# Attention and two feed-forward layers on one core: first chunk's scores in fp32, weight shifts given one half ahead, bit steps off the layer change

## The chip, the cores and the metric

One core of a Trainium2 chip runs the whole program. The metric is device time in microseconds (us), from the profiler's view of one execution; lower is better.

## The reference

```python
# _attn_ref: q, k, v are (4, 12, 448, 64), w_pre and w_post (12, 12)
scores = (1 / sqrt(64)) * matmul(q, k.transpose(0, 1, 3, 2))
scores = einsum('bhij,hg->bgij', scores, w_pre)
attn = exp(scores - max(scores, axis=-1)); attn = attn / (sum(attn, axis=-1) + 1e-09)
attn = einsum('bhij,hg->bgij', attn, w_post)
x = matmul(attn, v)                      # then to (1792, 768)
# _moe_ref: w_in (768, 2048), w_out (2048, 768)
h = x @ w_in; x = (h * cos(h)) @ w_out
# _moe2_ref: w_gate, w_val (768, 1536), w_out (1536, 768)
g = x @ w_gate; out = (g / (1 + exp(-g)) * (x @ w_val)) @ w_out
```

## The kernel before

**Attention.** Each of the four batches has its 448 query rows cut into four chunks of 12, 12, 11 and 10 blocks of ten rows. For a chunk, `qk` makes the scores of a pair of heads `m` (two heads, in rows 0 to 63 and 64 to 127 of the array) as three matmuls a head on values split into a rounded high part and a rest (type fp32r): `hi_q`, `lo_q`, `hi_k` and `lo_k` make these parts. `spread` copies each head's scores out of PSUM and sends them by DMA into `X`, where the partitions are ten rows times twelve heads, so that one matmul with a 120 by 120 matrix (`premix`, tile `psm`) mixes the heads of a block. Then come row maximum (`rowmax`, DVE), exponential (`expo`, ACT), normalization, the second mixing (`post`, tile `psa`) and, once a chunk is done, the product with v (`pv`, tile `psv`).

What a step does is written out by hand: a plan holds, for each block (a step), the functions to be called, and `ORDER` sorts them within a step. `QK_FIRST` and `V_FIRST` are steps of chunk 0, at which the pairs of heads of chunk 1 are scored and the four parts of v are loaded. Engines run their instructions in the order in which they are recorded, so an instruction that waits holds back all behind it on its engine.

Ahead of step 0 stands a start written out by hand: loads of K and q on SP's queue, splits, the scores of chunk 0, their copies, and the spreads. A spread of chunk 0 goes in two DMAs, the first for blocks 0 to 3 (`FIRST`), the second for blocks 4 to 11; SP and ACT issue them.

**Feed-forward.** A unit (layer, group of 256 hidden columns, quarter `t` of the tokens) makes its hidden values (`l1`, tiles `ph`; `hidden_a`, `hidden_b`) while the unit before it is multiplied into the output (`l2`, tiles `py`, six column blocks `m`). `acc` is summed by DVE, or copied by ACT in a layer's first group. Weights arrive as 64-bit numbers and are turned to fp32 halves: `w_shift` (ACT) scales the high words, three `w_bits` steps (DVE) put in the low ones, `w_split` (ACT and POOL) makes high part and rest. `w_steps` lists these; `fill(n)` runs the next n entries between the matmuls' other work. Halves of the out matrix and of the in matrices are two kinds of conversion, and a list of one kind (`what`) is followed by one of the other. At the end of layer 0 the maxima of `acc` give the scale of layer 1 (`next_max`, `next_unit`, `next_part`).

Of the kernel before, what the change touches and what calls it, by code (L numbers as in the profile page):

```python
# [7 lines left out]
F32 = mybir.dt.float32  # L8
F32R = mybir.dt.float32r
# [21 lines left out]
Q_STEPS = (-10, -6, -3)  # L31
K_STEPS = (1, 3, 5, 8, 10, 12)
V_STEPS = (4, 8, 12, 16)
QK_FIRST = (0, 0, 3, 3, 5, 5)
V_FIRST = (8, 10, 12, 14)
AT_DVE = (2, 5, 8)
ORDER = (
    "scale_v", "mixed_out", "l1_part", "norm_hi", "dma_v", "spread", "post", "rowmax", "w_sum",
# [16 lines left out]
def attention(ctx, tc, qT, kT, vN, mix, xs, ff):  # L55
    nc = tc.nc
# [27 lines left out]
    def bank(name):  # L84

        second = len(banks) % 4 > 1 or "closed" in banks
        banks.append(name)
        pool, tag = (ps_v, "pv") if second else (ps_s, "s")
        return pool.tile([128, 512], F32, tag=tag, name=name)
# [40 lines left out]
    def hi_k(b, m, copy=nc.scalar.copy):  # L130

        t = ktiles[b, m] = tuple(
            p_k.tile([128, S], F32R, tag=f"k{z}", name=f"k{z}_{b}_{m}") for z in range(2)
        )
        copy(t[0], raws["k", b, m])
# [5 lines left out]
    def dma_q(b, c, parts=(slice(0, 6),)):  # L141

        if parts[0].start == 0:
            qtiles[b, c] = tuple(
                p_q.tile([128, 6, 120], F32R, tag=f"q{z}", name=f"q{z}_{b}_{c}") for z in range(2)
            )
            raws["q", b, c] = p_q.tile([128, 6, 120], F32, tag="qr", bufs=2, name=f"qr_{b}_{c}")
        src = qT[b, c].rearrange("d (m i) -> d m i", m=6)
        for s in parts:
            nc.sync.dma_start(raws["q", b, c][:, s], src[:, s])  # L150
# [40 lines left out]

    X, SP, SMALL, PM, E, EHL, PA, AT, PV = ({} for _ in range(9))

    def qk(b, c, m, places=()):

        n = 10 * CH[c]
        for e in range(2):
            name = f"pss_{b}_{c}_{2 * m + e}"
            if places:
                pool, tag = places[(2 * m + e) % len(places)]  # L200
                SP[b, c, 2 * m + e] = pool.tile([128, 512], F32, tag=tag, name=name)
            else:
                SP[b, c, 2 * m + e] = bank(name)
        for i, (zq, zk) in enumerate(((0, 0), (1, 0), (0, 1))):
            for e in range(2):
                r = slice(64 * e, 64 * e + 64)
                nc.tensor.matmul(  # L207
                    SP[b, c, 2 * m + e][:n, :S], qtiles[b, c][zq][r, m, :n], ktiles[b, m][zk][r],
                    start=(i == 0), stop=(i == 2),
                )  # L210

    def spread_part(b, c, h, k0, k1):

        eng = nc.scalar if h % 2 else nc.sync
        eng.dma_start(X[b, c][h:120:12, k0:k1], raws["s", h][10 * k0:10 * k1])

    def spread(b, c, h, pool=p_s, bufs=None, copy=nc.scalar.copy):
# [166 lines left out]
    with tc.manual_schedule():  # L384
        vec, act, pl = nc.vector, nc.scalar, nc.gpsimd
        dma_k(0, 0, p_fk)
        dma_q(0, 0, (slice(0, 3),))
        dma_k(0, 1, p_fk)
        dma_q(0, 0, (slice(3, 6),))
        for m in range(2, 6):  # L390
            dma_k(0, m, p_fk)
        nc.sync.dma_start(mix_sb, mix)
        dma_q(0, 1)
        places = (ps_s, "s"), (ps_a, "a"), (ps_m, "m")
        for m in range(6):
            hi_k(0, m, act.copy if m % 2 else vec.tensor_copy)
            lo_k(0, m, pl if m % 2 else vec)
            if m < 2:
                hi_q(0, 0, m, act.copy)
                lo_q(0, 0, m, pl if m else vec)  # L400
        wpre_sb = const.tile([120, 120], F32, name="wpre_sb")
        nc.vector.tensor_scalar(wpre_sb, wpre_raw, SM, None, op0=ALU.mult)
        for m in range(6):
            qk(0, 0, m, places)
            for e in range(2):
                spread(0, 0, 2 * m + e, p_fk, 12, vec.tensor_copy if e else act.copy)
        for h in range(H):
            spread_part(0, 0, h, FIRST, CH[0])
        wm = p_small.tile([120, 1], F32, tag="wm", bufs=1, name="wm")
        nc.vector.tensor_reduce(out=wm, in_=wp, axis=AX.X, op=ALU.max, apply_absolute_value=True)  # L410
        wpost_sb = [const.tile([120, 120], F16, name=f"wpost{z}") for z in range(2)]
        first_k.close()
        p_at = pool("a_at", 2)
        p_o = pool("a_o", 3)
        pw = pow2_c(pow2_b(pow2_a(wm, 120, "w"), 120, "w"), 120, "w")
        nc.vector.tensor_scalar(wpost_sb[0], wp, pw[:120, 1:2], None, op0=ALU.mult)
        nc.vector.scalar_tensor_tensor(
            wpost_sb[1], wp, pw[:120, 1:2], wpost_sb[0], op0=ALU.mult, op1=ALU.subtract
        )
        for e in range(2):  # L420
            hi_q(0, 1, e)
            lo_q(0, 1, e)
        for i in range(-1, NB + 24):
            if i == first[B - 1, 3]:
                scores.close()
                banks.append("closed")
                ff.open_early()
            if i == NB + 1:
                mixed.close()
                ff.open_ps()  # L430
            for kind in ORDER:
                for fn, a in plan.pop((i, kind), []):
                    fn(*a)
# [3 lines left out]
class FeedForward:  # L437
# [180 lines left out]
    def w_steps(self):  # L618


        halves = lambda keys: [(key, z) for key in keys for z in range(2)]
        groups = [(L, g) for L in range(2) for g in range((FF1, FF2)[L] // 256)]
        outs = lambda L, g: [((L, "o", 2 * g + e), z) for z in range(2) for e in range(2)]
        seq = [("conv", outs(0, 0), 0, ("o", 0, 0))]
        for n in range(1, len(groups) + 1):
            for bi, batch in enumerate(self.batches(*groups[n]) if n < len(groups) else [()]):

                room = 4 * (n - 3) if n < 8 else 24 if n == 8 else 4 * (n - 1)
                if batch:
                    seq.append(("max", batch, room, None))  # L630
                if bi == 0 and n > 1:
                    seq.append(("conv", outs(*groups[n - 1]), 4 * (n - 2) + 1, ("o", *groups[n - 1])))
                if batch:
                    seq.append(("conv", halves(batch), room, ("i", *groups[n], bi)))
        self.to_load = []
        out = []
        for kind, what, room, name in seq:
            if kind == "max":
                hs = halves(what)
                for j, (key, z) in enumerate(hs):  # L640
                    out.append((room, None, [
                        *([(self.new_scale, what)] if j == 0 else []), (self.w_max, key, z),
                        *([(self.w_sum, what), (self.add_sum, what)] if j == 3 else []),
                    ]))
                continue
            self.to_load += what
            for j, (key, z) in enumerate(what):
                nxt = what[j + 1] if j + 1 < len(what) else None
                for k in range(3):
                    do = [(self.w_shift, key, z)] if j == k == 0 else []  # L650
                    do.append((self.w_bits, key, z, (k,)))
                    if k == 1 and nxt:
                        do.append((self.w_shift, *nxt))
                    if k == 2:
                        do += [(self.w_split, key, z), (self.load_next,)]
                    out.append((room, name if nxt is None and k == 2 else None, do, key))
        return out

    def add_sum(self, batch):
# [14 lines left out]
    def fill(self, n):  # L674

        while n and self.todo:
            room, name, do, *key = self.todo[0]
            if room > self.now or (key and any(key[0] in batch for batch in self.sums)):
                return
            self.todo.pop(0)  # L680
            for fn, *a in do:
                fn(*a)
            if name:
                self.done.add(name)
            n -= 1
# [162 lines left out]
    def steps(self):  # L848
# [7 lines left out]
        for i in range(1, len(seq) + 1):  # L856
# [31 lines left out]
                self.l1(0, 0, 2, 0)  # L888
            for m in range(6):
                self.l2(L0, g0, t0, m)  # L890
                if i == 1 and m == 0:
                    self.hidden(0, 0, 1, 1)
                if m == 0 and 1 < i < len(seq):
                    self.fill(1)
                    self.hidden_b(L, g, t, 1)
                    self.sum_up()
                if m in (1, 3) or i == 1 or (m == 5 and (L0 or i < 4)):
                    self.fill(1)
                if 0 <= t_max < 4 and m == 3:
                    self.next_unit(t_max)  # L900
                if 0 < m < 4 and 0 <= t_new < 4:
                    self.next_part(t_new, m + 2)
# [77 lines left out]
```

## Time and profile before

| | us |
|---|---|
| median of 3 runs | 1418.13 (1417.9 to 1418.47) |
| the profiled execution | 1418.45 |
| its span, first to last instruction | 1416.7 |
| PE matmuls busy in the span | 1385.8 (98%) |
| DVE, ACT, POOL busy | 993.4, 621.0, 469.5 |

The span is what the trace shows; 1.75 us of the execution lie outside it. PE's share counts a matmul's modelled duration, in which neighbours overlap, so 98% doesn't mean that PE works at its peak. Names such as `pss<-k,q` are output and inputs of an instruction; L207 is line 207 of the kernel; ACTq and SPq are the queues' own issue instructions, x12 the number of merged instructions.

### The profile page before, as it was taken

The numbers are of one execution on the slowest core, as the hardware profiler recorded it, in microseconds if no ns is written. First come the engines' busy times: TensorE is split into PE (matmuls) and PEld (weight loads), VectorE is DVE, ScalarE is ACT, GpSimd is POOL, SyncE is SP. The second block draws the span as 40 slices with busy tenths as digits, with TensorE's granted clock in tenths as the row PEclk, the third lists the DMA queues.
The fourth block names the chain that finished last, engine by engine and source line by source line (L and its number), as shares of the span: only waits on it lengthen the run. The fifth ranks groups of instructions, "written<-read, shape, count | busy, mean of one in ns | idle before, by whom it ended". The sixth has DMA issues, their size and how long they took to land.

```text
span 1416.7 us, 25084 instructions
## 1 busy us (share of the span) xinstructions
PE 1385.8 (98%) x9562; PEld 964.0 (68%) x9562; DVE 993.4 (70%) x2157; ACT 621.0 (44%) x1319; POOL 469.5 (33%) x499
## 2 busy tenths in 40 slices
PE   6899999999999999999999999999999999999998
PEld 3577777777776776767676767656666666666666
DVE  4977887877879667878887878875555466465523
ACT  3776776777665543333333333455422232232210
POOL 2454454453423332333242333343322222231310
PEclk9999999999999999999999999999999999999999
DMA  5554554554547222221121221021212122120012
GB/s 175 153 155 129 153 157 127 165 156 119 162 121 246 56 68 67 67 68 56 57 78 56 58 77 45 23 67 46 78 35 66 46 61 74 45 78 12 1 47 111
DMA packets 100209, 126.16 MB, mean 89 GB/s; under 512 B 29592, under 2 KB 88440, under 8 KB 100088
## 3 DMA queue, kind: packets, MB, share of 16 engines
q1 hardware_dynamic: 99248, 123.26, 29.4%
q8 instruction: 75, 1.23, 0.4%
q10 hardware_dynamic: 840, 1.29, 0.3%
q14 instruction: 46, 0.38, 0.1%
HBM read 75.45 MB, written 10.37 MB: 61 GB/s over the span
## 4 chain that ended last, share of the span: by engine, by line
PE 83%; DVE 9%; DMA 3%; ACT 2%; issue 2%; ACTq 1%; POOL 0%; SPq 0%; DVEq 0%; POOLq 0%
PE ph L718 12%; PE ph L720 12%; PE ph L719 12%; PE py L768 9%; PE py L769 8%; PE py L770 8%; PE psm L232 8%; PE psv L306 4%; PE pss L207 4%; PE psa L281 2%; PE psa L282 2%; PE psa L283 2%; DMA x<-s 2%; DVE el L268 1%; DVE sm L237 1%
## 5 line engine op out<-in xcount | busy, mean ns | idle before, releaser
L718 PE MATMUL ph<-x,h_i 128*128 128x448 f16 x960 | 338.7, 353 | 0.0
L720 PE MATMUL ph<-x,l_i 128*128 128x448 f16 x960 | 338.3, 352 | 0.0
L719 PE MATMUL ph<-x,h_i 128*128 128x448 f16 x960 | 338.3, 352 | 0.0
L774 DVE TENSOR_TENSOR acc<-py,acc 128x448 f32<-128x448 f32 x288 | 177.5, 620 | 143.0 <-PE py L770 133.7
L753 POOL TENSOR_TENSOR gl<-r,gh 128x448 fp32r<-128x448 f32 x112 | 135.0, 1205 | 401.7 <-ACT gh L752 398.1
L768 PE MATMUL py<-gh,h_o 128*128 128x448 f32 x672 | 254.7, 379 | 6.9 <-DVE acc L774 4.8
L769 PE MATMUL py<-gl,h_o 128*128 128x448 f32 x672 | 243.9, 363 | 0.0
L770 PE MATMUL py<-gh,l_o 128*128 128x448 f32 x672 | 243.6, 362 | 0.0
L261 POOL TENSOR_SCALAR eh<-e,sm 120x448 f16<-120x448 f32 x180 | 122.0, 678 | 245.3 <-DVE sm L256 155.2
L232 PE MATMUL psm<-x,wpre_sb 120*120 120x448 f32 x360 | 179.6, 582 | 4.5 <-ACT e L245 4.2
L718 PEld LDWEIGHTS <-h_i 128*128 128x128 f16 x960 | 93.8, 98 | 91.2 <-issue 8.8
L245 ACT ACTIVATE e<-psm,sm 120x448 f32<-120x448 f32 x180 | 114.8, 638 | 89.3 <-DVE sm L237 81.0
L720 PEld LDWEIGHTS <-l_i 128*128 128x128 f16 x960 | 93.9, 98 | 87.6
L719 PEld LDWEIGHTS <-h_i 128*128 128x128 f16 x960 | 94.0, 98 | 82.2 <-issue 0.3
L768 PEld LDWEIGHTS py<-gh,h_o 128*128 128x128 f32 x672 | 126.3, 188 | 24.5 <-DVE acc L774 8.2
L237 DVE TENSOR_REDUCE sm<-psm 120x1 f32<-120x448 f32 x180 | 111.0, 617 | 41.9 <-PE psm L232 41.7
L751 DVE SCALAR_TENSOR_TENSOR r<-ph,by_i,r 128x448 f32<-128x448 f32 x112 | 76.3, 681 | 90.4 <-PE ph L720 73.6
L752 ACT CAST gh<-r 128x448 fp32r<-128x448 f32 x112 | 63.5, 567 | 164.9 <-DVE r L751 164.2
L268 DVE SCALAR_TENSOR_TENSOR el<-e,sm,eh 120x448 f16<-120x448 f32 x180 | 135.6, 753 | 0.0
L770 PEld LDWEIGHTS py<-gh,l_o 128*128 128x128 f32 x672 | 126.1, 188 | 8.9
L769 PEld LDWEIGHTS py<-gl,h_o 128*128 128x128 f32 x672 | 126.3, 188 | 7.5
L592 POOL TENSOR_TENSOR l_i<-f_i,h_i 128x384 f16<-128x384 f32 x80 | 78.1, 976 | 160.0 <-ACT h_i L591 160.0
(102 smaller groups left out, 2235.7 us busy)
## 6 DMA issues: line engine op xcount, KB each, us to landing
r_o<-in_w_out SPq DMA_DIRECT2D x56, 384.0 KB
x<-s SPq DMA_DIRECT2D x84, 210.0 KB
r_i<-in_w_in SPq DMA_DIRECT2D x32, 384.0 KB
x<-s SPq DMA_DIRECT2D x48, 192.5 KB
r_i<-in_w_gate SPq DMA_DIRECT2D x24, 384.0 KB
r_i<-in_w_val SPq DMA_DIRECT2D x24, 384.0 KB
x<-s SPq DMA_DIRECT2D x48, 175.0 KB
qr<-in_qT SPq DMA_DIRECT2D x15, 360.0 KB
```

The source lines that it names most:

```text
L232: nc.tensor.matmul(ps[:120, :S], wpre_sb, X[b, c][:120, k], start=True, stop=True)
L237: nc.vector.tensor_reduce(out=sm[:, 0:1], in_=PM[b, c, k][:120, :S], axis=AX.X, op=ALU.max, negate=True)
L261: nc.gpsimd.tensor_scalar(eh, E[b, c, k], sm[:, 3:4], 1.0, op0=ALU.mult, op1=ALU.mult)
L268: nc.vector.scalar_tensor_tensor(el, E.pop((b, c, k)), sm[:, 3:4], eh, op0=ALU.mult, op1=ALU.subtract)
L718: nc.tensor.matmul(ps, wh, xh, start=(kk == 0), stop=False)
L719: nc.tensor.matmul(ps, wh, xl, start=False, stop=False)
L720: nc.tensor.matmul(ps, wl, xh, start=False, stop=(kk == 5))
L753: nc.gpsimd.tensor_tensor(gl, r, f(gh), op=ALU.subtract)
L768: nc.tensor.matmul(ps, wh, gh[:, e], start=(e == 0), stop=False)
L769: nc.tensor.matmul(ps, wh, gl[:, e], start=False, stop=False)
L770: nc.tensor.matmul(ps, wl, gh[:, e], start=False, stop=(e == 1))
L774: nc.vector.tensor_tensor(acc, ps, acc, op=ALU.add)
```

## The change

1. The scores of chunk 0 of batch 0 are made by a new `qk_first` from the raw q and K, one fp32 matmul a head in place of three fp32r ones. The splits of that chunk's q are gone. Those of K stay for the later chunks: all high parts on DVE, all rests on POOL.
2. In the start, scores, K's high part and copies follow each other pair by pair. ACT issues the spreads that it copied itself (even heads), SP those of DVE. The split of chunk 1's q comes ahead of the scale of `w_post`.
3. The pairs of chunk 1 are scored at steps 1, 4 and 7 in place of 0, 3 and 5; the first load of v is recorded at step 11 in place of 8.
4. In `w_steps`, the shift of the next half is given at the second bit step also where the next half is of the other kind.
5. In units that follow the last of layer 0 (`0 <= t_max < 4`) no `fill` stands after `m` 1 and 3.
6. In the first unit `hidden(0, 0, 1, 1)` is cut in two, `hidden_a` behind block 0 and `hidden_b` behind block 3.

```diff
-QK_FIRST = (0, 0, 3, 3, 5, 5)
-V_FIRST = (8, 10, 12, 14)
+QK_FIRST = (1, 1, 4, 4, 7, 7)
+V_FIRST = (11, 12, 13, 14)
...
+    def qk_first(m, places):
+
+        for e in range(2):
+            pool, tag = places[(2 * m + e) % len(places)]
+            ps = SP[0, 0, 2 * m + e] = pool.tile([128, 512], F32, tag=tag, name=f"pss_0_0_{2 * m + e}")
+            r = slice(64 * e, 64 * e + 64)
+            nc.tensor.matmul(
+                ps[:120, :S], raws["q", 0, 0][r, m], raws["k", 0, m][r], start=True, stop=True
+            )
...
-        eng = nc.scalar if h % 2 else nc.sync
+        eng = nc.sync if h % 2 else nc.scalar
...
         for m in range(6):
-            hi_k(0, m, act.copy if m % 2 else vec.tensor_copy)
-            lo_k(0, m, pl if m % 2 else vec)
-            if m < 2:
-                hi_q(0, 0, m, act.copy)
-                lo_q(0, 0, m, pl if m else vec)
+            qk_first(m, places)
+            hi_k(0, m, vec.tensor_copy)
+            for e in range(2):
+                spread(0, 0, 2 * m + e, p_fk, 12, vec.tensor_copy if e else act.copy)
+            lo_k(0, m)
...
+                    if k == 1:
+                        nxt = self.to_load[n] if n < len(self.to_load) else None
+                        given = nxt and (not last or nxt[0][1] == "o" or seq[si + 1][0] == "conv")
+                        if given:
+                            keys.append(nxt[0])
+                            do.append((self.w_shift, *nxt))
...
-                if i == 1 and m == 0:
-                    self.hidden(0, 0, 1, 1)
+                if i == 1 and m in (0, 3):
+                    (self.hidden_b if m else self.hidden_a)(0, 0, 1, 1)
...
-                if m in (1, 3) or i == 1 or (m == 5 and (L0 or i < 4)):
+                if m in (1, 3) and not 0 <= t_max < 4 or i == 1 or (m == 5 and (L0 or i < 4)):
                     self.fill(1)
```

ACT at the start of the program, before (`s_0_2` is the copied score of chunk 0, head 2; `10x4x448` is the first DMA of a head, `10x8x448` the second):

```order
L135 CAST k_0_5_164<-kr_5_133 128x448
L223 COPY s_0_0_179<-pss_0_0_170 120x448
L215 DMA x_0_178<-s_0_1_182 10x4x448
L223 COPY s_0_2_193<-pss_0_2_185 120x448
L215 DMA x_0_178<-s_0_3_196 10x4x448
```

and of the change:

```order
L229 ACT_TABLE_LOAD
L229 COPY s_0_0_146<-pss_0_0_138 120x448
L221 DMA x_0_145<-s_0_0_146 10x4x448
L229 COPY s_0_2_160<-pss_0_2_153 120x448
L221 DMA x_0_145<-s_0_2_160 10x4x448
```

Five casts ahead of the first copy are gone, and each DMA now follows a copy of ACT's own.

ACT where the conversions pass from an in matrix to an out matrix in layer 0, before (`f_i`, `f_o` are halves in work, `py_0_2_3` is group 0, quarter 2, block 3; `hpi` marks the sine):

```order
L772 COPY acc_7798<-py_0_2_1_8108 128x448
L772 COPY acc_7798<-py_0_2_2_8117 128x448
L772 COPY acc_7798<-py_0_2_3_8125 128x448
L591 CAST h_i_3_0_8063<-f_i_3_1_8057 128x384
L772 COPY acc_7798<-py_0_2_4_8138 128x448
L772 COPY acc_7798<-py_0_2_5_8146 128x448
L741 ACTIVATE r_1_0_0_8183<-r_1_0_0_8183,hpi 128x448
L553 ACTIVATE f_o_0_8188<-r_o_0_7806 128x384
```

and of the change:

```order
L779 COPY acc_7768<-py_0_2_1_8078 128x448
L555 ACTIVATE f_o_0_8087<-r_o_0_7776 128x384
L779 COPY acc_7768<-py_0_2_2_8089 128x448
L779 COPY acc_7768<-py_0_2_3_8097 128x448
L593 CAST h_i_3_0_8033<-f_i_3_1_8027 128x384
L779 COPY acc_7768<-py_0_2_4_8110 128x448
L779 COPY acc_7768<-py_0_2_5_8118 128x448
L748 ACTIVATE r_1_0_0_8155<-r_1_0_0_8155,hpi 128x448
```

The shift of the first out half (`f_o_0`) stands ahead of the last in half's cast now, and no longer behind the next unit's sine.

DVE in the last unit of layer 0 (group 7, quarter 3), before (`f_o` steps are bit steps of weights, `mx` the maxima, `sx` the sum over partitions that `next_unit` reads):

```order
L774 TENSOR_TENSOR acc_7799<-py_7_3_1_12006,acc_7799 128x448
L778 TENSOR_REDUCE mx_11998<-acc_7799 128x1
L567 SCALAR_TENSOR_TENSOR f_o_1_11933<-r_o_1_11278,f_o_1_11933 128x384
L774 TENSOR_TENSOR acc_7799<-py_7_3_2_12024,acc_7799 128x448
L778 TENSOR_REDUCE mx_11998<-acc_7799 128x1
L774 TENSOR_TENSOR acc_7799<-py_7_3_3_12037,acc_7799 128x448
L778 TENSOR_REDUCE mx_11998<-acc_7799 128x1
L561 TENSOR_SCALAR f_o_1_12001<-f_o_1_12001 128x384
L796 TENSOR_SCALAR mx_11789<-sx_12047 128x1
```

and of the change:

```order
L781 TENSOR_TENSOR acc_7769<-py_7_3_1_11976,acc_7769 128x448
L785 TENSOR_REDUCE mx_11968<-acc_7769 128x1
L781 TENSOR_TENSOR acc_7769<-py_7_3_2_11989,acc_7769 128x448
L785 TENSOR_REDUCE mx_11968<-acc_7769 128x1
L781 TENSOR_TENSOR acc_7769<-py_7_3_3_12002,acc_7769 128x448
L785 TENSOR_REDUCE mx_11968<-acc_7769 128x1
L803 TENSOR_SCALAR mx_11761<-sx_12011 128x1
```

The two bit steps between the sums have moved to the next unit.

## Rows read from the trace of the kernel before

**Rows 1.** the page: the span of the profiled execution

```profile
span 1416.7 us, 25084 instructions
```

**Rows 2.** waits of PE: for whom, us in total, times, longest

```profile
PE py L768 <- DVE acc L774: 4.8, 7, 0.9
PE py L768 <- ACT acc L772: 1.9, 3, 1.3
```

**Rows 3.** timeline of ACT: start, us, what, [idle before <-releaser]

```profile
3.79 0.49 ACT L154 CAST q<-qr 128x360 fp32r<-128x360 f32 x1 [1.77 <-DMA qr<-in_qT]
9.19 0.56 ACT L135 CAST k<-kr 128x448 fp32r<-128x448 f32 x1 [1.38 <-DMA kr<-in_kT]
13.85 0.78 ACTq L215 DMA_DIRECT2D x<-s  x1
17.73 8.06 ACTq L215 DMA_DIRECT2D x<-s  x7
25.84 1.84 ACT L223 COPY s<-pss 120x448 f32<-120x448 f32 x4 [7.87 <-DMA x<-s]
```

**Rows 4.** timeline of PE, start of the program

```profile
24.40 3.34 PE L232 MATMUL psm<-x,wpre_sb 120*120 120x448 f32 x4
32.41 1.76 PE L232 MATMUL psm<-x,wpre_sb 120*120 120x448 f32 x4
34.11 1.47 PE L207 MATMUL pss<-k,q 64*120 64x448 f32 x12
```

**Rows 5.** chain that ended last, mixing of the heads

```profile
254.12 4.27 PE psv L306 x96
```

**Rows 6.** timeline of DVE at the start: two casts of K

```profile
3.36 0.39 DVE L135 CAST k<-kr 128x448 fp32r<-128x448 f32 x1 [2.10 <-DMA kr<-in_kT]
8.91 1.32 DVE L135 CAST k<-kr 128x448 fp32r<-128x448 f32 x1
```

**Rows 7.** timeline of PE: mix of the first block of chunk 1

```profile
48.05 1.01 PE L232 MATMUL psm<-x,wpre_sb 120*120 120x448 f32 x2
```

**Rows 8.** timeline of ACT while chunk 0 is mixed

```profile
30.89 0.63 ACT L245 ACTIVATE e<-psm,sm 120x448 f32<-120x448 f32 x1 [1.73 <-DVE sm L237]
37.85 0.53 ACT L223 COPY s<-pss 120x448 f32<-120x448 f32 x1 [0.71 <-DMA x<-s]
```

**Rows 9.** timeline of DVE in chunk 1: a maximum over v

```profile
49.90 0.93 DVE L169 TENSOR_REDUCE vmx<-v 112x1 f32<-112x768 f32 x1
```

**Rows 10.** chain that ended last, at a chunk's end

```profile
169.89 4.53 DMA x<-s
```

**Rows 11.** timelines of PE and ACT, first unit of the feed-forward part

```profile
474.59 0.47 PE L768 MATMUL py<-gh,h_o 128*128 128x448 f32 x1 [1.31 <-ACT acc L772]
...
473.54 0.56 ACT L752 CAST gh<-r 128x448 fp32r<-128x448 f32 x1 [0.75 <-DVE r L751]
```

**Rows 12.** timelines of DVE (two) and PE where a shift comes late

```profile
526.92 0.74 DVE L561 TENSOR_SCALAR f_i<-f_i 128x384 int32<-128x384 int32 x1 [0.58 <-ACT f_i L553]
...
556.47 0.36 DVE L561 TENSOR_SCALAR f_o<-f_o 128x384 int32<-128x384 int32 x1 [0.70 <-ACT f_o L553]
...
558.00 0.47 PE L768 MATMUL py<-gh,h_o 128*128 128x448 f32 x1 [0.71 <-DVE acc L774]
```

**Rows 13.** timelines of DVE and PE at the change of layer

```profile
920.87 1.15 DVE L567 SCALAR_TENSOR_TENSOR f_o<-r_o,f_o 128x384 int32<-128x384 int32 x1
924.30 0.76 DVE L561 TENSOR_SCALAR f_o<-f_o 128x384 int32<-128x384 int32 x1
...
922.60 0.47 PE L768 MATMUL py<-gh,h_o 128*128 128x448 f32 x1 [0.28 <-DVE acc L774]
925.18 0.16 PE L533 MATMUL su_i<-u_i,ones 128*128 128x2 bf16 x1 [1.10 <-DVE mx L796]
```

**Rows 14.** one stretch: its us, then busy PE, PEld, DVE, ACT, POOL

```profile
560.00:700.00 140.00, 139.29 (x718) 100.63 (x717) 115.99 (x223) 49.14 (x88) 47.29 (x44) 1.00 0.24 68
```

**Rows 15.** timeline of ACT: a shift that waits for POOL

```profile
913.32 0.56 ACT L553 ACTIVATE f_o<-r_o 128x384 f32<-128x384 f32 x1 [2.10 <-POOL l_o L592]
```

More of the change, by code (lines that the diff above doesn't have):

```diff
@@ L143, in dma_q @@
         if parts[0].start == 0:
-            qtiles[b, c] = tuple(
-                p_q.tile([128, 6, 120], F32R, tag=f"q{z}", name=f"q{z}_{b}_{c}") for z in range(2)
-            )
+            if b + c:
+                qtiles[b, c] = tuple(
+                    p_q.tile([128, 6, 120], F32R, tag=f"q{z}", name=f"q{z}_{b}_{c}") for z in range(2)
+                )
             raws["q", b, c] = p_q.tile([128, 6, 120], F32, tag="qr", bufs=2, name=f"qr_{b}_{c}")
@@ L192, in attention, with qk @@
     X, SP, SMALL, PM, E, EHL, PA, AT, PV = ({} for _ in range(9))
-    def qk(b, c, m, places=()):
+    def qk_first(m, places):
[5 more added lines that the diff above has]
+                ps[:120, :S], raws["q", 0, 0][r, m], raws["k", 0, m][r], start=True, stop=True
+            )
+    def qk(b, c, m):
         n = 10 * CH[c]
         for e in range(2):
[L198 to L203, printed above, removed]
+            SP[b, c, 2 * m + e] = bank(f"pss_{b}_{c}_{2 * m + e}")
         for i, (zq, zk) in enumerate(((0, 0), (1, 0), (0, 1))):
@@ L395, in attention @@
         for m in range(6):
-            hi_k(0, m, act.copy if m % 2 else vec.tensor_copy)
-            lo_k(0, m, pl if m % 2 else vec)
-            if m < 2:
-                hi_q(0, 0, m, act.copy)
-                lo_q(0, 0, m, pl if m else vec)
+            qk_first(m, places)
[3 more added lines that the diff above has]
+            lo_k(0, m)
         wpre_sb = const.tile([120, 120], F32, name="wpre_sb")
         nc.vector.tensor_scalar(wpre_sb, wpre_raw, SM, None, op0=ALU.mult)
[L403 to L406, printed above, removed]
         for h in range(H):
             spread_part(0, 0, h, FIRST, CH[0])
+        for e in range(2):
+            hi_q(0, 1, e)
+            lo_q(0, 1, e)
         wm = p_small.tile([120, 1], F32, tag="wm", bufs=1, name="wm")
@@ L419, in attention @@
         )
-        for e in range(2):
-            hi_q(0, 1, e)
-            lo_q(0, 1, e)
         for i in range(-1, NB + 24):
@@ L634, in w_steps @@
                     seq.append(("conv", halves(batch), room, ("i", *groups[n], bi)))
-        self.to_load = []
-        out = []
-        for kind, what, room, name in seq:
+        self.to_load = [half for kind, what, *_ in seq if kind == "conv" for half in what]
+        out, n, given = [], 0, False
+        for si, (kind, what, room, name) in enumerate(seq):
             if kind == "max":
@@ L645, in w_steps @@
                 continue
-            self.to_load += what
             for j, (key, z) in enumerate(what):
-                nxt = what[j + 1] if j + 1 < len(what) else None
+                n += 1
                 for k in range(3):
-                    do = [(self.w_shift, key, z)] if j == k == 0 else []
+                    keys = [key]
+                    last = j == len(what) - 1
+                    do = [] if given or k else [(self.w_shift, key, z)]
                     do.append((self.w_bits, key, z, (k,)))
-                    if k == 1 and nxt:
-                        do.append((self.w_shift, *nxt))
+                    if k == 1:
[4 more added lines that the diff above has]
+                            do.append((self.w_shift, *nxt))
                     if k == 2:
                         do += [(self.w_split, key, z), (self.load_next,)]
-                    out.append((room, name if nxt is None and k == 2 else None, do, key))
+                    out.append((room, name if last and k == 2 else None, do, *keys))
         return out
@@ L676, in fill @@
         while n and self.todo:
-            room, name, do, *key = self.todo[0]
-            if room > self.now or (key and any(key[0] in batch for batch in self.sums)):
+            room, name, do, *keys = self.todo[0]
+            if room > self.now or any(key in batch for key in keys for batch in self.sums):
                 return
```

## The prediction

> **What bounds the kernel now.** I read the page first: the span is 1416.7 us [rows 1], and PE is busy nearly throughout. So an edit pays only where PE waits or runs slowly. The waits of PE come next. In the feed-forward part its output matmuls (L768) wait for the sums of DVE seven times, 4.8 us in all, and for the copies of ACT three times, 1.9 us [rows 2]. With the 1.1 us in which the sum matmul of a weight scale stands behind the layer change [rows 13], that is 7.8 us, and it is all that edits 4 to 6 can give back. The rest of what the change touches is the start.
>
> There the timelines say what ends last. ACT has the first half of q at 3.79 us and the last block of K at 9.19 [rows 3]; the inputs are all there early. But from 17.73 to 25.79 ACT's queue does nothing except issue seven spreads, 1.15 us each, and the copies behind them begin at 25.84 [rows 3]. The exponentials of chunk 0 stand behind those copies. The first block of chunk 1 is mixed at 48.05 [rows 7]. From 25.84 to there are 22.2 us, in which ACT again stands idle, for example 1.73 us for a row maximum and 0.71 us for a spread that still holds a buffer [rows 8]. After 48 us the same work follows in the same order, on PE; I take the whole rest to move with that moment.
>
> One more view belongs to the start, the matmul durations. Two mixes take 3.34 us at 24.40 and 1.76 us at 32.41 [rows 4]. So PE runs at the lower of its two levels, 1.2 GHz, up to about 32 us, and at 2.4 GHz after it.
>
> **Start: scores in fp32.** A pair is two fp32 matmuls over 64 rows, which no row of before shows. The nearest ones: an fp32 mix of the same 448 columns takes 1.67 us at the lower level and 0.88 at the upper (half of [rows 4]). Whether the two halves of a pair run side by side is open. In fp32r they do: twelve matmuls of 448 columns in 1.47 us [rows 4] are 0.12 us each, where one alone at 2.4 GHz needs 448/2.4 = 0.187. In fp32 the product with v, two heads in two halves of the columns, takes 4.27 us for 96 records, that is 48 matmuls of 120 columns [rows 5]; scaled from the mix (0.88 us for 448 columns) they would need 11.3 us one by one. Both rows speak for side by side. So a pair costs 1.67 us (bounds 0.88, and 3.34 if one by one).
>
> The Trainium skill ("TensorEngine Tiling (Array Packing)", Key Properties) says the same: tiles of the array work independently, but a change of the tiling mode drains the engine. By it the switch from pairs to the full-height matmuls that follow would cost one drain, as it did before the change.
>
> The first pair can start at 3.8 us. Six at 1.67 us end at 13.8; with the upper level from the middle on, 3.8 + 3 x 1.67 + 3 x 0.88 = 11.5. Then ACT copies the last even head (0.46 us, a quarter of the 1.84 of [rows 3]) and issues its spread (0.78 us): 12.7 to 15.1, middle 13.9. Its six second spreads follow, at 1.15 us each 6.9 us. **ACT is free at 20.8 us (19.6 to 22.0) in place of 25.84: 5.0 us (3.8 to 6.2).** The first block's maximum isn't later: a spread lands within 4.53 us [rows 10], so the last first part at 14.3 + 4.5 = 18.8; with a mix at 1.67 and a maximum at about 0.6 (block rows of DVE) that is 21.1, just beside 20.8.
>
> The splits that go (q) and move (K) lie beside this. A cast of K takes 0.39 us on DVE when nothing runs on POOL, and 1.32 us when POOL subtracts beside it [rows 6]. Each DVE turn of cast and copy is then 0.39 + 0.6 = 1.0 us, or 1.9 us. The first hides behind a pair of 1.67 us; the second doesn't, and six turns of it would end at 3.4 + 11.4 = 14.8 in place of 14.3, which costs 0.5 us. I take nothing, since POOL subtracts only what DVE has cast, so that a rest runs mostly beside a copy from PSUM. The Trainium skill ("GPSIMD Engine Reference", Specifications) speaks against the change here: POOL shares its SBUF interfaces with VectorE and contends with instructions in a two-port mode, and all six rests are on POOL now. The trace agrees as to size (0.39 against 1.32); by the rule alone all casts would be slow, and the sum 0.5 us smaller.
>
> **From ACT's freedom to chunk 1.** The same work remains, except that the four first copies now stand behind the first exponential. What can go are the waits: the pairs of chunk 1 come at steps 1, 4 and 7, evenly, so a buffer is no longer asked for before its spread has landed (0.71 us here), and PE, at work on scores from 5 us on, should reach the upper level before 32 us, which shortens the 1.73 us. Bounds 0 and 4, taken 2.0, less than the 2.4 of the two rows. Against it stands the load of v: its four maxima, 0.93 us each [rows 9], fall on four steps in a row in place of every second one. The SP queue's order isn't changed by step 11; the DMAs have landed anyway. DVE has some slack over chunk 1, so 0 to 1.9 us, taken 0.3. **Start: 5.0 + 2.0 - 0.3 = 6.7 us.**
>
> **First unit, edit 6.** PE waits 1.31 us for a copy of ACT, because the cast of `gh`, queued ahead of that copy, waits 0.75 us for DVE [rows 11]. With `hidden_b` behind block 3, two copies go ahead of the cast. The sine stays ahead, so a little of the wait remains: 1.2 us (0.7 to 1.9, all of ACT's waits). What `hidden_b` feeds is needed only in the next unit, behind 18 matmuls.
>
> **Shifts, edit 4.** The hand-overs between kinds are 25; four of them meet a moment at which DVE has nothing else. There its bit step waits 0.58 or 0.70 us for ACT's shift, the hidden values behind it are late, the sum behind those too, and PE waits 0.71 us [rows 12]. Two more such pairs, near 656 and 755 us, read as the second does. With the shift one half ahead these waits go: 0.58 + 3 x 0.70 = 2.7 us (0 if ACT stands elsewhere then, up to DVE's 4.8 [rows 2] less the next term).
>
> **Layer change, edit 5.** Bit steps of 1.15 and 0.76 us stand between sums; PE waits 0.28 us for the next sum and 1.10 us for the maxima read behind the second [rows 13]. Without them 1.4 us (0 to 1.9). The steps then stand in the next unit, where DVE waits for PE.
>
> **The sum** is 6.7 + 1.2 + 2.7 + 1.4 = 12.0 us. The profiled execution has 1418.45 us, 0.3 above the median; against the median 1418.1 - 12.0 = **1406.1 us**.
>
> **Rivals.** *One by one:* the halves of a pair don't overlap. Against it speak [rows 4, 5]. With the upper level from the third pair on, 3.8 + 2 x 3.34 + 4 x 1.76 = 17.5, then 0.46 + 0.78 + 6.9: ACT is free at 25.6, and the start gives 0.2 + 2.0 - 0.3 = 1.9 us; total 7.2, 1411. With no rise of the clock 3.8 + 20.0 + 8.1 = 31.9: 6.1 lost, the whole 0.9 slower, 1419.
>
> *The shifts don't pay:* what DVE waited for it waits for still, in another instruction. Then only the start and edits 5 and 6 give: 9.3 us, 1408.8; with none of edits 4 to 6, 1411.4.
>
> *Late spreads of chunk 1:* its last copies stand at step 8 of 12, two steps later than before. A spread needs up to 4.53 us from issue to landing and then is the chain that ends last [rows 10]. If PE waits for it at step 12, up to 3 us are given back: 1409.
>
> *Slower:* a shift given ahead needs one of two buffers that POOL frees. At 913 us ACT waits 2.10 us for that [rows 15], and all behind it on ACT, `gh` and copies, waits too. If each of the 25 hand-overs put 0.5 us on PE: 12.5 lost, 2.7 not gained, 9.3 gained, 1418.1 + 3.2 = 1421. It decides from 9.3/25 = 0.37 us each. Against it: shifts inside a kind are given just so already, and from 560 to 700 us PE is busy 139.29 of 140 us [rows 14].
>
> **How the numbers follow.** Less than 0.2% (2.8 us) can't be told from no change here. Forecast, 1401 to 1410: 0.68. One by one: 0.10, of it 0.02 slow enough to be the same. The shifts don't pay: 0.09. Late spreads: 0.06. Slower: 0.04; no effect at all for reasons I don't see: 0.03, split into same and slower. Faster is then 0.92, same 0.04, slower 0.04. The low end, 1400, is all upper bounds of the start (6.2 + 4 = 10.2) and some 8 us of waits; the high end, 1412, takes in the first two rivals. About 0.08 lie above it and 0.06 below.
>
> **What would show it.** Right: ACT's first copy of chunk 1 or first exponential at 20 to 22 us; a pair of fp32 scores with two starts nearly together; the first mix of chunk 1 near 41 us; no wait of bit steps for ACT near 550, 650 and 750 us (earlier by the start); PE's waits for DVE's sums below 2.5 us, the one before the scale's sum gone. Wrong: second spreads that take longer on a fuller queue, since the inputs and spreads now meet; PE at 1.2 GHz long into chunk 0; a wait of PE for DVE in chunk 1 as large as what the start gave.

## The result and the profile after

| | before | changed |
|---|---|---|
| median of 5 runs, us | 1418.29 (1417.9 to 1421.75) | 1405.65 (1404.97 to 1407.2) |
| ratio to before, 95% interval | | 0.9909 [0.9895, 0.9922] |
| the profiled execution, its span | 1418.45, 1416.7 | 1407.2, 1405.4 |
| first exponential (ACT) | 27.54 | 21.90 |
| first mix of chunk 1 (PE) | 48.05 | 43.96 |
| first and last output matmul | 467.42, 1412.71 | 463.50, 1401.46 |
| feed-forward part between these | 945.29 | 937.96 |

The kernel became 12.6 us faster, 0.9%; 1406.1 was forecast. The profiled execution is the longest of the five, 1.55 us above the median.

The start in ACT's timeline (start, us, what, idle before and what ended it):

```profile
5.73 0.53 ACT L229 COPY s<-pss 120x448 f32<-120x448 f32 x1 [3.71 <-PE pss L201]
...
13.24 0.53 ACT L229 COPY s<-pss 120x448 f32<-120x448 f32 x1 [0.85 <-ACT s L229]
13.80 8.04 ACTq L221 DMA_DIRECT2D x<-s  x7
21.90 0.63 ACT L251 ACTIVATE e<-psm,sm 120x448 f32<-120x448 f32 x1 [8.13 <-DMA x<-s]
```

ACT is done issuing at 21.84, where [rows 3] had 25.79; now the first exponential comes next, and no copy stands ahead of it. The same stretch in PE's timeline, and SP's queue:

```profile
3.87 6.98 PE L201 MATMUL pss<-kr,qr 64*120 64x448 f32 x24 [3.87 <-DMA qr<-in_qT]
15.39 0.75 PE L105 MATMUL psp_w<-diag_w,ones 120*128 120x120 f32 x2 [4.54 <-DVE diag_w L100]
17.17 1.82 PE L238 MATMUL psm<-x,wpre_sb 120*120 120x448 f32 x2 [1.02 <-DMA x<-s]
...
43.96 0.98 PE L238 MATMUL psm<-x,wpre_sb 120*120 120x448 f32 x2 [2.21 <-DMA v<-in_vN]
...
45.41 1.78 PE L238 MATMUL psm<-x,wpre_sb 120*120 120x448 f32 x2
```

```profile
27.91 10.70 SPq L231 DMA_DIRECT2D x<-s  x8
38.66 2.11 SPq L163 DMA_DIRECT2D v<-in_vN  x4
```

The twelve fp32 matmuls of the scores take 6.98 us, so the halves of a pair run side by side (one by one, at the 0.88 us of a mix at 2.4 GHz, they would need 10.6); in the trace the two start 0.01 to 0.03 us apart. The first mix of chunk 1 then waits 2.21 us. The row names the load of v, but this matmul reads `x`: its last spread is issued at 38.61, v right behind it, and by the semaphore updates in the trace that spread lands at 43.72. Against [rows 7] the mix comes 4.1 us earlier, where 7.0 were forecast. And the mix behind it (one matmul, recorded as two) takes 1.78 us. The stretches (us, busy PE, PEld, DVE, ACT, POOL, granted clock, DMA share, GB/s) say why:

```profile
15.00:22.00 7.00, 5.58 (x18) 3.01 (x18) 2.40 (x9) 0.10 (x1) 1.07 (x2) 0.53 0.61 193
22.00:44.00 22.00, 16.94 (x131) 10.37 (x129) 16.51 (x46) 15.71 (x41) 9.37 (x13) 1.00 0.65 191
44.00:49.00 5.00, 5.00 (x32) 3.42 (x34) 3.18 (x9) 1.91 (x5) 0.99 (x3) 0.66 0.78 210
```

Twice PE waits some microseconds and then works at 1.2 GHz for a while: at the end of the 4.54 us before 15.39 and on from there, and behind the 2.21 us before 43.96.

In the feed-forward part PE's waits up to 900 us, and the two places of [rows 11] and [rows 13], now read (PE's rows):

```profile
PE py L775 <- DVE acc L781: 1.5, 2, 0.9
PE py L775 <- ACT acc L779: 0.5, 1, 0.5
```

```profile
467.90 0.47 PE L775 MATMUL py<-gh,h_o 128*128 128x448 f32 x1 [0.47 <-ACT acc L779]
...
914.60 0.16 PE L535 MATMUL su_i<-u_i,ones 128*128 128x2 bf16 x1
```

From 900 to 970 us no wait of PE is left. Up to 900 us bit steps wait for a shift 5 times in place of 16, and not at all from 490 to 850 us, as here on DVE:

```profile
549.26 0.35 DVE L563 TENSOR_SCALAR f_o<-f_o 128x384 int32<-128x384 int32 x1
```

The part is 7.3 us shorter, where 5.3 were forecast. So the sum was right by two errors that nearly cancel, and the experiments ask about both.

### The profile page after: what moved, and what is told of

Its sections match the earlier page's. It is cut to its first block, busy times and chain, and to the rows that moved or that the text cites. A ratio compares the mean times of both kernels' runs of the same rounds, so it can differ in the third digit from the quotient of the medians.

```text
span 1405.4 us, 25058 instructions
## 1 busy us (share of the span) xinstructions
PE 1379.4 (98%) x9550; PEld 960.8 (68%) x9550; DVE 990.4 (70%) x2156; ACT 618.6 (44%) x1314; POOL 471.7 (34%) x501
## 4 chain that ended last, share of the span: by engine, by line
PE 90%; DVE 5%; ACT 1%; DMA 1%; issue 1%; ACTq 1%; POOL 0%; SPq 0%; DVEq 0%; POOLq 0%
PE ph L725 13%; PE ph L727 12%; PE ph L726 12%; PE py L775 9%; PE py L776 9%; PE py L777 9%; PE psm L238 9%; PE psv L312 5%; PE pss L213 4%; PE psa L287 2%; PE psa L289 2%; PE psa L288 2%; DVE el L274 1%; DVE sm L243 1%; DMA qr<-in_qT 1%
```

## The experiments

Ratios are to the kernel before, run on the same chip, with 95% intervals. "Theory A" and "B" are those of each expectation.

**1. The parts alone, on the kernel before.** Four kernels: edits 1 to 3 without the feed-forward edits; edits 4 to 6 alone; edit 4 alone (`w_steps` and `fill` as in the diff ahead of the prediction); edit 5 alone:

```diff
-                if m in (1, 3) or i == 1 or (m == 5 and (L0 or i < 4)):
+                if m in (1, 3) and not 0 <= t_max < 4 or i == 1 or (m == 5 and (L0 or i < 4)):
```

Edits 1 to 3: 

> Edits 1 to 3 alone; the feed-forward part is that of before. Theory A (read from the trace after: the start gives 4.0 us at the first mix of chunk 1, the feed-forward edits 7.3): 4.0 us faster than before, about 1414.3, and the first output matmul of the feed-forward part near 463.5 as in the trace after. Theory B (the prediction's terms, start 6.7 and the feed-forward edits 5.3): 1411.6. If the wait before the first mix of chunk 1 and the stretch at 1.2 GHz behind it come from the start's own order, both stand here too, near 42 to 44 and 45 to 49 us.

Edits 4 to 6: 

> Edits 4 to 6 alone; the start is that of before. Theory A: 7.3 us faster, about 1411.0. Theory B: 5.3 us faster, 1413.0. Rival, a part of the 7.3 is not the edits' own but the clock's or an unrelated difference between two executions: between 5 and 6.5 us. The feed-forward part from its first output matmul to its last should take 938.0 us as in the trace after under A, 940.0 under B, where before takes 945.3.

Edit 4: 

> Edit 4 alone, shifts given one half ahead across kinds. Theory A: the four late shifts give 3.4 us and a little at the layer change, 1414.5. Theory B (the prediction's term): 2.7 us, 1415.6. Rival of the prediction, the shifts don't pay: 1418.3, with the waits of bit steps still there or moved to another instruction. The late sum before the output matmuls near 527, 558, 656 and 756 us should be gone; the one near 550 may leave 0.1.

Edit 5: 

> Edit 5 alone, no fill after m 1 and 3 in the units after the last of layer 0. Theory A: 2.3 us faster, 1416.0 (waits of 0.3 near 922.6, of 1.1 ahead of the scale's sum and of some 0.9 behind the change go). Theory B (the prediction's term): 1.4 us, 1416.9. Rival: the bit steps are late in the next unit, nothing is gained, 1418.3.

| kernel | median, us | ratio | first to last output matmul, us |
|---|---|---|---|
| edits 1 to 3 | 1412.47 | 0.996 [0.9948, 0.9972] | 945.33 |
| edits 4 to 6 | 1410.31 | 0.9947 [0.9935, 0.9959] | 938.27 |
| edit 4 | 1413.56 | 0.997 [0.996, 0.9981] | 941.02 |
| edit 5 | 1415.75 | 0.9986 [0.9977, 0.9996] | 942.89 |
| before, same chip | 1417.88 | | 945.29 (first profile) |

The start gives 5.4 us and the feed-forward edits 7.6, together 13.0; both theories had one of the two wrong: the start is between 4.0 and 6.7. The profile of edits 1 to 3 has the wait ahead of chunk 1 (1.82 us, first mix at 42.58) and the stretch at 1.2 GHz behind it as well, so both come from the start's own order. The last column leaves the start out: 7.0 us for the three edits, 4.3 for edit 4, 2.4 for edit 5. In edit 4's kernel PE's first unit still waits as in [rows 11], with all three edits that wait is gone (PE's timelines, edit 4 first, then edits 4 to 6):

```profile
470.95 0.47 PE L773 MATMUL py<-gh,h_o 128*128 128x448 f32 x1 [0.45 <-ACT acc L777]
473.74 0.47 PE L773 MATMUL py<-gh,h_o 128*128 128x448 f32 x1 [1.32 <-ACT acc L777]
```

```profile
471.08 0.47 PE L773 MATMUL py<-gh,h_o 128*128 128x448 f32 x1 [0.45 <-ACT acc L777]
```

For a finer account I set the 2016 starts of output matmuls of two traces side by side, each counted from its first. The changed kernel gains 1.30 us in the first unit (edit 6), 1.13, 0.76, 0.76 and 0.76 in the 5th, 7th, 14th and 21st (edit 4, and the same places in its kernel alone), 1.74 in the 32nd, the last of layer 0 (edit 5), and 0.61 in the 33rd. This last gain appears with edit 4 alone (0.53) and with edit 5 alone (0.51): either one suffices. Before, two output matmuls start 0.29 us late there, one behind a copy of ACT; why either edit mends it stayed open.

PE's waits up to 900 us in edit 5's kernel are those of [rows 2] (4.5 of 4.8 us for DVE fall there), in edit 4's 1.5:

```profile
PE py L768 <- DVE acc L774: 4.5, 6, 0.9
```

```profile
PE py L773 <- DVE acc L779: 1.5, 2, 0.9
```

**2. fp32 alone, on the kernel before.** `qk_first` in place of `qk(0, 0, m, places)`, without `hi_q` and `lo_q` of that chunk:

```diff
-            qk(0, 0, m, places)
+            qk_first(m, places)
```

> The kernel before with the first chunk's scores in fp32 and no split of its q; splits of K, copies and spreads stand in the order of before. Theory A, the order in which ACT and DVE work is what held ACT back and fp32 alone gives little: the casts and rests of K still stand ahead of DVE's copies to 11.6 us, six copies of 0.6 us follow, ACT's last copy ends near 15.5 and its seven issues near 23.5; the first exponential near 23.6 in place of 25.8, 2.2 us or less faster. Theory B, the matmuls were the bound: all of the 4.0 us at the first exponential come from fp32, near 21.9.

1417.87 us, 0.9999 [0.9991, 1.0008]: nothing. (A single profile says less: this one begins chunk 1 at 46.77, 1.3 us earlier than before, but then takes 946.74 us from the first to the last output matmul, where the same code before took 945.29; PE falls to 1.2 GHz there once, at 472 us behind the wait of [rows 11].) ACT, then DVE:

```profile
13.32 0.53 ACT L233 COPY s<-pss 120x448 f32<-120x448 f32 x1 [3.31 <-DVE s L233]
...
17.98 7.84 ACTq L225 DMA_DIRECT2D x<-s  x7
25.86 1.84 ACT L233 COPY s<-pss 120x448 f32<-120x448 f32 x4 [8.02 <-DMA x<-s]
```

```profile
8.83 1.44 DVE L139 TENSOR_TENSOR k<-kr,k 128x448 fp32r<-128x448 f32 x1
10.19 1.14 DVE L409 TENSOR_SCALAR wpre_sb<-mix_sb 120x120 f32<-120x120 f32 x1
11.26 1.67 DVE L233 COPY s<-pss 120x448 f32<-120x448 f32 x3
```

DVE's first copy still stands behind the rests of K, to 11.26; ACT issues spreads of DVE's copies and waits for them; it is free at 25.86, as before to 0.02 us. My 23.5 was too early: the score banks stay full until DVE copies, and PE makes its last five score matmuls only from 11.92 on, in 5.33 us, at 1.2 GHz (granted clock 0.50 from 11.5 to 32 us). So theory A holds more strongly than I put it: in the old order fp32 gives nothing. That it pays because the scores no longer need the splits, so that the order of edit 2 becomes possible, is the reading this leaves; it isn't shown, since no run has that order without fp32, and the clock has a part in the late copies here.

**3. The wait before chunk 1.** Three changes of the changed kernel: v two steps later; the last pairs at step 6; all loads of v behind the first spreads of chunk 2.

```diff
-V_FIRST = (11, 12, 13, 14)
+V_FIRST = (13, 14, 15, 16)
```

> The changed kernel with the loads of v two steps later (13, 14, 15, 16). Theory A, v's 1.4 MB, issued right behind the last spread of chunk 1, share the DMA engines with it: PE's wait of 2.21 us ahead of chunk 1's first mix falls by 1 us or more, and with it the stretch at 1.2 GHz behind it goes, 1.5 us: 1 to 3 us faster than the changed kernel. Theory B, the spread is late by its own issue (37.85 to 38.61) and takes its 4.5 us anyway: wait unchanged within 0.3 us, time unchanged.

```diff
-QK_FIRST = (1, 1, 4, 4, 7, 7)
+QK_FIRST = (1, 1, 4, 4, 6, 6)
```

> The changed kernel with the last two pairs of chunk 1 scored at step 6 in place of 7. Theory A (late spreads): the last spread is issued some 1.5 us earlier, the wait of 2.21 us ahead of chunk 1's first mix falls to about 0.7 us, and the stretch at 1.2 GHz goes or shrinks: 1.5 to 3 us faster than the changed kernel. Theory B (buffers): the copies then stand behind spreads that still hold the six buffers, ACT waits instead and the exponentials are as much later: no change.

```diff
-V_FIRST = (11, 12, 13, 14)
+V_FIRST = (13, 14, 15, 16)
...
-                at(v0, dma_v, b, jc)
+                at(v0 if b else V_FIRST[3], dma_v, b, jc)
```

> The changed kernel with all four loads of v recorded at step 16, behind the first spreads of chunk 2, and the maxima at steps 17 to 20: on SP's queue no load of v follows chunk 1's last spread directly. Theory A, v's traffic delays that spread: PE's wait ahead of chunk 1's first mix (2.21 us in the changed kernel, 1.85 with two of the four loads behind it) falls to 1 us or less. Theory B, the spread is issued too late and takes its 4.5 to 5 us: the wait stays at 1.5 to 2.2 us.

PE at chunk 1's first mix, in this order:

```profile
42.76 0.98 PE L238 MATMUL psm<-x,wpre_sb 120*120 120x448 f32 x2 [1.85 <-DMA v<-in_vN]
```

```profile
40.39 1.01 PE L238 MATMUL psm<-x,wpre_sb 120*120 120x448 f32 x2
```

```profile
41.65 0.98 PE L238 MATMUL psm<-x,wpre_sb 120*120 120x448 f32 x2 [0.90 <-DMA qr<-in_qT]
...
57.54 1.83 PE L238 MATMUL psm<-x,wpre_sb 120*120 120x448 f32 x2 [2.57 <-ACT e L251]
```

Pairs at 6: the wait is gone, the mix is at 40.39 (the prediction's "near 41"), 1403.51 us, 0.9897 [0.9882, 0.9912]; theory A. Its last spread is issued at 35.13 in place of 38.61. So the step of the last pair made the wait.

v late: 1403.14 us, 0.9895 [0.9882, 0.9909], but the wait only fell to 1.85; theory A's condition failed, and my reason for a gain with it. The gain is elsewhere: chunk 1 takes 29.1 us from its first mix to chunk 2's, where pairs at 6 takes 30.8 (and the changed kernel, with its fall to 1.2 GHz, 31.9). With pairs at 6 the matmul of v's scale waits 0.8 us on PE, and the scores behind it another 1.0; with v late only 0.7 us of both is left.

v behind: PE starts 4.35 us after the last spread's issue, where the changed kernel needs 5.35 (edits 1 to 3 alone 4.97, v late, with two of the loads behind it, 5.00). So v's traffic costs that spread some 0.6 to 1.0 us, by one execution each; theory A. The kernel is no faster (1405.91, 0.9915 [0.9901, 0.993]): all maxima of v come late, and at 57.54 PE waits 2.57 us and falls to 1.2 GHz.

**4. ACT's issues.** Heads 8 and 10 get their second spread from SP:

```diff
-        eng = nc.sync if h % 2 else nc.scalar
+        eng = nc.sync if h % 2 or (k0 and h > 7) else nc.scalar
```

> The changed kernel with ACT's last two second spreads (heads 8 and 10) issued by SP. Theory A, ACT's issue block (13.80 to 21.84) is what holds the first exponential: it comes 2.3 us earlier, near 19.6, where the first maximum ends too, and the first mix of chunk 1 1 to 2 us earlier. Theory B, from the first exponential on the mixes wait for the second spreads or the later copies all the same: PE waits for a spread at block 4, and chunk 1's first mix is where it was, near 44.

```profile
20.52 0.64 ACT L251 ACTIVATE e<-psm,sm 120x448 f32<-120x448 f32 x1 [6.00 <-DVE sm L243]
...
24.11 0.63 ACT L251 ACTIVATE e<-psm,sm 120x448 f32<-120x448 f32 x1 [0.76 <-DVE sm L243]
```

```profile
22.28 1.89 PE L238 MATMUL psm<-x,wpre_sb 120*120 120x448 f32 x4
...
44.02 0.98 PE L238 MATMUL psm<-x,wpre_sb 120*120 120x448 f32 x2 [1.88 <-DMA v<-in_vN]
```

The first exponential comes 1.4 us earlier and now waits for DVE's maximum instead of a spread, yet chunk 1 starts at 44.02: theory B, 1405.75 us, 0.9911 [0.9897, 0.9925]. The gain is lost long before the late spread: the second exponential comes at 24.11, in the changed kernel at 24.20. It waits for the maximum of a mix that PE makes only at 22.28, behind the first scores of chunk 1.

**5. Edit 3 undone.**

```diff
-QK_FIRST = (1, 1, 4, 4, 7, 7)
-V_FIRST = (11, 12, 13, 14)
+QK_FIRST = (0, 0, 3, 3, 5, 5)
+V_FIRST = (8, 10, 12, 14)
```

> The changed kernel with edit 3 undone: pairs of chunk 1 at steps 0, 0, 3, 3, 5, 5 and v at 8, 10, 12, 14. Theory A (late spreads: edit 3 costs what it was to bring): no wait of PE for chunk 1's spreads, first mix near 41, 2 us faster than the changed kernel, about 1403.5. Theory B (the prediction's: evenly set pairs take waits for buffers off ACT): ACT waits again for a spread that holds a buffer, first mix at 44 or later, 0 to 2 us slower than the changed kernel.

```profile
22.21 1.84 ACT L229 COPY s<-pss 120x448 f32<-120x448 f32 x4 [8.34 <-DMA x<-s]
```

```profile
42.99 1.01 PE L238 MATMUL psm<-x,wpre_sb 120*120 120x448 f32 x2
```

1405.07 us, 0.9909 [0.9894, 0.9924]: neither theory, the same as the changed kernel. Four copies stand ahead of the first exponential again (23.91), PE waits 2.24 us ahead of a mix at 24.73, and no spread is late at 42.99. Edit 3 as a whole moved the loss and removed nothing.

**6. Put together.** Pairs at 6 and v late; then also ACT's two spreads on SP.

> The changed kernel with the last pairs of chunk 1 at step 6 and the loads of v at 13 to 16. Theory A, the two gain in different places (pairs at 6: the first mix of chunk 1 at 40.4 in place of 44.0; v late: chunk 1 from its first mix to chunk 2's in 29.1 us in place of 30.8, since the scale of v no longer stops PE for 0.8 and 1.0 us): first mix at 40.4, chunk 2's at 69.5, 1401.5 us. Theory B, both only remove the same late spread and its stretch at 1.2 GHz: no faster than the better of the two, 1403.

> As the kernel with pairs at 6 and v late, and ACT's last two second spreads issued by SP. Theory A, with the late spread out of the way the earlier first exponential (20.5 in place of 21.6) reaches chunk 1: first mix of chunk 1 near 39.4, 1 us faster than without. Theory B, block 0's own spreads and mix bound the first exponential and SP's longer queue delays the second parts: no faster, 0 to 0.5 us slower.

1403.07 us, 0.9892 [0.9875, 0.9908], and 1402.37 us, 0.9892 [0.9877, 0.9907]. PE and SP's queue of the first, then PE of the second:

```profile
35.52 1.46 PE L238 MATMUL psm<-x,wpre_sb 120*120 120x448 f32 x2 [1.84 <-ACT e L251]
...
44.02 0.98 PE L238 MATMUL psm<-x,wpre_sb 120*120 120x448 f32 x2 [0.89 <-DMA qr<-in_qT]
```

```profile
27.30 8.34 SPq L231 DMA_DIRECT2D x<-s  x8
```

```profile
40.78 1.01 PE L238 MATMUL psm<-x,wpre_sb 120*120 120x448 f32 x2
```

In the first, ACT's copies wait four times for a spread that holds a buffer (at most 1.03 us), PE waits 1.84 us and falls to 1.2 GHz (the mix of 1.46): chunk 1 starts at 44.02, not 40.4. Behind this stand slow spreads: the last one is issued at 35.64 and, by the semaphore updates in the trace, lands at 43.77, 8.1 us later (with pairs at 6 alone 39.96, 4.8 us). Why the spreads of this execution took so long stays open. This execution is the longest of its four (1401.88 to 1404.54), but a gain on top of either part isn't shown. The second starts chunk 1 at 40.78, not at the 39.4 of theory A, and chunk 2 at 70.5. Its four executions (1401.82 to 1404.31) lie below all five of the changed kernel (1404.97 to 1407.2). It is the fastest version here by the median, 3.3 us below the changed kernel; the intervals of the two ratios overlap, and that it is faster than pairs at 6 with v late isn't shown.

## Why the prediction was right, and where it was not

The sum is nearly the measured gain, but its terms are not: by the medians of the parts the start gave 5.4 us for 6.7 and the feed-forward edits 7.6 for 5.3. That the two errors nearly cancel is luck.

*ACT free, 5.0 us forecast, 4.0 measured (21.84 for 20.8).* The mechanism holds: pairs side by side and issues as the block ahead of the first exponential. Two sizes were off. The last even copy starts at 13.24, since ACT's own turn of copy and issue (1.38 us a pair) sets the pace, and not PE's pairs, which end at 10.86. And seven issues take 8.04 us, 0.36 more than 0.78 + 6 x 1.15 (7.40 with edits 1 to 3 alone). A pair was sized well: up to 7.7 us it takes 1.49 us from start to start, from 8.8 us on 0.75, for the forecast 1.67 and 0.88. In one thing the forecast of the first exponential was too small: it came 5.6 us earlier, because the four copies behind [rows 3]'s 25.84 no longer precede it.

*From ACT's freedom to chunk 1, 2.0 us forecast, 0.1 measured.* This step failed: 21.84 to 43.96 is 22.1 us, as long as before (with edits 1 to 3 alone 21.4). The rival "late spreads" came true, with 2.21 us of its "up to 3"; the prediction gave it 0.06. With pairs at 6 the same stretch takes 18.9 us (21.5 to 40.4), a gain of 3.3, inside the bounds of 0 and 4. I read the evenly set pairs as waits that go, and didn't follow the last pair through copy, SP's queue and landing to step 12. I had the 4.53 us of [rows 10] for that and used them for the rival only; the last spread here needed 5.35 us from issue to mix.

*The clock.* The prediction counted on 2.4 GHz earlier than at 32 us; it came at about 8 us, but PE then fell back twice. The second fall lies in chunk 1: 31.9 us there, against 30.6 before and 30.8 with pairs at 6, where it doesn't fall. The profiled start gives only 3.9 us by the first output matmul, while the medians give 5.4 for edits 1 to 3. The falls alone don't explain that: the profile of edits 1 to 3 falls behind the same two waits (chunk 1 takes 32.0 us) and begins the output matmuls at 462.27, 5.15 us earlier than before. Part of the difference lies ahead of chunk 1, which it begins 1.4 us earlier than the changed kernel's profile. The kernel before falls once too, at 431 us (granted clock 0.91 from 420 to 440 us), so one profile against another is good to a microsecond or two. For the start of the kernel before, a window shows a granted clock of 1.00, because its trace has no clock record ahead of 32 us; the level there is read from the durations in [rows 4].

*The bunched maxima of v, -0.3 us.* Fair in size: PE waits 0.8 us ahead of the matmul of v's scale, at 61.01, in place of 0.3. But the row names a copy of ACT, and DVE's part ends at 60.85; how much of the wait is the maxima's isn't shown.

*Casts beside POOL, taken as nothing.* Three of the six casts on DVE are slow (0.69 to 1.00 us); the second and the last:

```profile
6.31 0.38 DVE L135 CAST k<-kr 128x448 fp32r<-128x448 f32 x1
...
11.57 1.00 DVE L135 CAST k<-kr 128x448 fp32r<-128x448 f32 x1
```

The second has no rest beside it, the last runs while POOL subtracts. The Trainium skill ("GPSIMD Engine Reference", Specifications) says that POOL shares its SBUF interfaces with VectorE and contends with its instructions in a two-port mode or with two inputs in SBUF. The rows agree with contention for these three casts; no row shows a cast's mode. But DVE's last copy still ends at 13.1, ahead of ACT's at 13.8, so nothing was right for the sum.

*Feed-forward, 5.3 us forecast, 7.3 measured: mis-sized.* Edit 6 gave 1.30 (1.2), edit 4 3.4 (2.7), edit 5 1.74 and with edit 4 another 0.6 (1.4). The waits were read rightly; I counted them by the idle time in the rows. A matmul that starts after a wait lasts 0.47 us in its row, the others 0.36, and neighbours overlap. From start to start the wait of 1.31 us of [rows 11] costs 1.47 over the usual 0.20, 0.71 costs 0.87, 1.10 costs 1.26: 0.16 more each, and with seven waits (one of edit 6, four of edit 4, two of edit 5) 1.1 of the 2.0 us. For the first late shift I had also taken DVE's 0.58 us and not PE's 0.87.

*The other rivals.* One by one: fell, 6.98 us for twelve matmuls. The shifts don't pay: fell, edit 4 alone gives 4.3. Slower: no shift given ahead put a wait on PE. One sum among the rivals has the wrong sign: with no rise of the clock, 6.1 us lost against 2.0 - 0.3 and 5.3 gained make 0.9 us faster, 1417.2, and not 0.9 slower, 1419.

## What to carry to other kernels

A step that is moved later must be followed to its last consumer: copy, queue, landing; the price of a late spread was nearly all of the waits that the even placing saved. Waits of a pipelined engine are costed from start to start, since the idle time in a row leaves out what the broken overlap adds. And a wait near the start can cost twice, once itself and once in the clock behind it.

## What was not expected of the hardware

Two waits of PE, 4.54 and 2.21 us, each went over into a stretch at 1.2 GHz, in which one mix took 1.8 us in place of 1.0. The same wait need not have the same price: of four waits of 1.82 to 1.88 us near chunk 1 in the versions tried, two were followed by such a fall (edits 1 to 3 alone; pairs at 6 with v late) and two were not (v late; ACT's issues on SP). A load of 1.4 MB issued behind a spread went with 5.0 to 5.35 us from issue to mix in place of 4.35, and in one execution a spread took 8.1 us to land.
